# Attention and two expert layers on one core: two places for tokens that are transposed by DMA, some attention weights by DMA, and an order solved anew

## The chip, the cores and the metric

The kernel runs on one core of a Trainium2 chip. The metric is device time in microseconds from the start to the end of one execution. Runs of the kernel before took 1227.68 to 1228.92 us, with a median of 1227.95 us (3 runs).

## The reference, cut to what matters

```python
def _attn_ref(q, k, v):                    # (8, 8, 576, 64) each
    q_c, k_c, v_c = (x.reshape(8, 8, 9, 64, 64) for x in (q, k, v))     # chunks of 64 positions
    scores = 1.0 / np.sqrt(64) * np.matmul(q_c, k_c.transpose(0, 1, 2, 4, 3))
    attn = np.exp(scores - np.max(scores, axis=-1, keepdims=True))
    attn = attn / (np.sum(attn, axis=-1, keepdims=True) + 1e-09)
    return np.matmul(attn, v_c)            # reshaped to x, (4608, 512)

def _moe_ref(x, w_in, w_out, g_ln):        # w_in (512, 1024), w_out (1024, 512)
    h = x @ w_in
    e = np.exp(h - np.max(h, axis=-1, keepdims=True))
    solu = h * e / (np.sum(e, axis=-1, keepdims=True) + 1e-09)
    mu = np.mean(solu, axis=-1, keepdims=True)
    var = np.mean((solu - mu) ** 2, axis=-1, keepdims=True)
    return ((solu - mu) / np.sqrt(var + 1e-06) * g_ln) @ w_out

def _moe2_ref(x, w_in, w_out):             # w_in (512, 2048), w_out (2048, 512)
    h = x @ w_in
    return (h / (1.0 + np.exp(-h))) @ w_out
```

The three are applied one after the other. Inputs of the attention are 32-bit floats; the weights of the two layers arrive as 64-bit floats.

## The kernel before

**Two stages.** The first stage computes the attention and the first layer for 36 tiles of 128 rows, called tokens here and numbered from 0. The second stage computes the second layer by a scheme of seven products (`p1` to `p7`) instead of eight, for 6 groups of 768 rows: first its input product (336 `product` steps), then its output product (168 `out_product` steps). Every 32-bit operand is split into a high and a low part, and each product runs three passes (`PASSES`).

**One token in the first stage.** `attend(t)` (L556) multiplies token t's weights with its values and computes the scores of token t + 2; both go into the single `sx` tile in PSUM. ScalarE and VectorE split the attention result into `xs` (L607, L609). `weigh` (L582) turns scores into weights: maximum, difference, exponential, sum, a POOL multiplication (L596), then four TensorE transposes into `pp` (L600) and a copy to `pT` (L603). `moe_in` (L633) computes the 1024 columns of h in two halves of 12 matmuls; the PSUM tile `h` has one place. `hold` copies h to SBUF for the tokens that `HELD` marks (H), so that the place comes free. `norm` (L650) makes the normalised `u` in eight instructions, of which the last is L675.

**Turning a token.** The output product needs u transposed, as `lnT`, high and low. `turn_ln` (L677) does it with two groups of four TensorE transposes into `tp` (L683) and a split of each. `turn_x` (L688) does it for the 24 tokens that `XBAR` marks: a POOL copy takes the 16-bit halves of the words apart (L691), a transposing DMA follows (L694), a VectorE copy joins the halves (L697), and the split fills `lnT`. Each of its three buffers has one place, so tokens go through one behind the other. Four tokens make a block; `moe_out` (L704) computes the block's output in eight halves of 12 matmuls (`yp`), which are stored to DRAM as `y1d`.

**Weights.** `convert` (L486) turns 64-bit floats into 32-bit ones by integer operations: a scaling of the high word (on VectorE or ScalarE by `SCALE_ON`, L464, L466), a shift (L468) and two combinations (L470, L472). Pieces 0 to 7 are the first layer's weights, 8 to 23 the second layer's, which POOL mixes (L533) and SP stores. `LOW_ON` sets the engine of each low part; E is a subtraction by TensorE (L479, L480).

**What sets the order.** `stage_one` and `stage_two` describe every step with an engine, a length, needs, places and a due time. `Steps.solve` lists them by rank on each engine. The instructions are then issued in that order, and each engine, with SP for all DMAs, works through its queue in order. Tables of numbers at the end of the file (due times `FIRST`, `WAY_OUT`, `START`; engines) feed it.

```python
        pp = ps.tile([128, HP, 128], F32, tag="tr", name="pp", bufs=2)
        for hp in range(HP):
            nc.tensor.transpose(pp[:, hp, :], e[:, hp, :, :].rearrange("p h k -> p (h k)"), ident)
```

## Time and profile before

| | |
|---|---|
| median of 3 runs | 1227.95 us |
| the profiled execution | 1228.68 us |
| its span, first to last instruction | 1226.8 us |
| TensorE (PE) busy | 1187.6 us, 97% |
| VectorE (DVE) busy | 815.3 us, 66% |
| ScalarE (ACT) busy | 615.7 us, 50% |
| GpSimd (POOL) busy | 535.5 us, 44% |
| DMA | 257.31 MB, mean 210 GB/s |
| mean granted clock of TensorE | 0.992 |

Busy times are unions over an engine's instructions. The first product of the second stage starts at 504.72 us; from 527.6 us on TensorE runs second-stage products only.

### The profile page before, as it was taken

Reading aid. Unit: us, or ns where it says so; the run is one execution under the profiler, and the core shown is the slowest. Engines: PE = TensorE matmul, PEld = TensorE weight load, DVE = VectorE, ACT = ScalarE, POOL = GpSimd, SP = SyncE. Lnnn points to the kernel's source line nnn. Section 1 sums busy time; section 2 is a strip of 40 time slices with the busy share of each in tenths; the row PEclk is TensorE's granted clock in tenths of the full one; section 3 lists DMA queues with packets and bytes.
Section 4 is the critical chain, followed back from the end, with each engine's and each line's share of the span. In section 5 each row is a group of like instructions: output and inputs, shape, how many; then the busy total and the mean of one; then the engine's idle time right before and its main releaser. Section 6 shows DMA issues by size and latency. Waiting matters only on the chain.

```text
span 1226.8 us, 22015 instructions
## 1 busy us (share of the span) xinstructions
PE 1187.6 (97%) x8310; PEld 1093.5 (89%) x8310; DVE 815.3 (66%) x1119; ACT 615.7 (50%) x947; POOL 535.5 (44%) x510
## 2 busy tenths in 40 slices
PE   4999999898999999999999999999999999999998
PEld 2777778787888787899999999999999999999998
DVE  7987887887887865647565656566676555555553
ACT  4687545544555555654353435346655444444441
POOL 2344456455564642657667667578950000000000
PEclk9999999998999999999999999999999999999999
DMA  9444557758677653375757575659998777777772
GB/s 366 141 136 145 168 174 236 201 173 233 188 228 206 196 136 120 121 247 191 259 180 256 180 255 188 232 183 334 315 302 284 215 215 214 217 210 218 228 210 87
DMA packets 187177, 257.31 MB, mean 210 GB/s; under 512 B 64704, under 2 KB 142528, under 8 KB 187072
## 3 DMA queue, kind: packets, MB, share of 16 engines
q1 hardware_dynamic: 187072, 255.91, 67.0%
q8 instruction: 65, 1.06, 0.4%
q14 instruction: 40, 0.33, 0.1%
HBM read 143.66 MB, written 99.61 MB: 198 GB/s over the span
## 4 chain that ended last, share of the span: by engine, by line
PE 87%; DVE 6%; ACT 2%; DMA 2%; POOL 1%; issue 1%; SPq 0%; POOLq 0%; DVEq 0%
PE hyw L838 16%; PE hyw L926 16%; PE yp L710 13%; PE h L617 12%; PE h L838 12%; PE h L926 12%; PE sx L568 1%; DMA qk<-in_qk_dram 1%; PE sx L575 1%; DVE lnT L609 1%; DVE st L654 1%; PE tp L683 1%; DVE work L470 1%; PE pp L600 1%; DMA w2d<-work 1%
## 5 line engine op out<-in xcount | busy, mean ns | idle before, releaser
L912 DVE TENSOR_TENSOR gs<-gs 128x768 fp32r<-128x768 f32 x168 | 167.7, 1004 | 135.1 <-ACT gs L910 134.9
L910 ACT ACTIVATE gs<-gs 128x768 fp32r<-128x768 f32 x168 | 142.7, 849 | 176.5 <-PE hyw L926 82.5
L710 PE MATMUL yp<-lnT,wo 128*128 128x512 f32 x864 | 216.7, 400 | 3.8 <-DVE lnT L609 3.8
L617 PE MATMUL h<-wi,xs 128*128 128x512 f32 x864 | 216.8, 401 | 2.7 <-DVE u L660 1.7
L838 PE MATMUL hyw<-y1s,w2t 128*128 128x384 f32 x1152 | 214.6, 336 | 0.0
L926 PE MATMUL hyw<-gs,w2o 128*128 128x384 f32 x1152 | 211.5, 335 | 0.0
L838 PEld LDWEIGHTS hyw<-y1s,w2t 128*128 128x128 f32 x1152 | 202.0, 188 | 0.2
L926 PEld LDWEIGHTS hyw<-gs,w2o 128*128 128x128 f32 x1152 | 201.6, 188 | 0.0
L617 PEld LDWEIGHTS h<-wi,xs 128*128 128x128 f32 x864 | 162.3, 191 | 39.7 <-PE sx L575 1.7
L710 PEld LDWEIGHTS yp<-lnT,wo 128*128 128x128 f32 x864 | 162.4, 191 | 38.5 <-DVE lnT L609 4.5
L885 POOL TENSOR_TENSOR work<-work 128x384 f32<-128x384 f32 x144 | 161.1, 1139 | 76.2 <-ACT work L880 64.0
L838 PE MATMUL h<-y1s,w2t 128*128 128x384 f32 x864 | 164.5, 335 | 0.0
L926 PE MATMUL h<-gs,w2o 128*128 128x384 f32 x864 | 161.2, 336 | 0.0
L838 PEld LDWEIGHTS h<-y1s,w2t 128*128 128x128 f32 x864 | 151.7, 188 | 0.3
L926 PEld LDWEIGHTS h<-gs,w2o 128*128 128x128 f32 x864 | 151.1, 188 | 0.0
L596 POOL TENSOR_TENSOR e<-e,sm 128x512 f32<-128x512 f32 x36 | 51.2, 1423 | 59.9 <-DVE sm L594 53.8
L852 DVE TENSOR_TENSOR work<-hyw,work 128x384 f32<-128x384 f32 x48 | 26.7, 556 | 58.5 <-PE hyw L838 58.0
L533 POOL TENSOR_TENSOR work<-work 128x256 f32<-128x256 f32 x64 | 55.7, 888 | 20.0 <-DVE work L472 15.7
L864 ACT ACTIVATE work<-work 128x384 f32<-128x384 f32 x48 | 25.1, 524 | 77.8 <-DVE work L862 77.5
L672 POOL TENSOR_TENSOR st<-st,nhalf 128x1 f32<-128x1 f32 x36 | 33.0, 916 | 68.0 <-DVE st L670 67.6
L885 DVE TENSOR_TENSOR work<-work 128x384 f32<-128x384 f32 x48 | 49.3, 1034 | 14.9 <-POOL work L885 14.9
L675 ACT ACTIVATE u<-u,st 128x1024 f32<-128x1024 f32 x36 | 44.8, 1245 | 24.9 <-POOL st L673 24.9
(100 smaller groups left out, 1442.4 us busy)
## 6 DMA issues: line engine op xcount, KB each, us to landing
gd<-work SPq DMA_DIRECT2D x336, 192.0 KB, 2.3
gs<-gd SPq DMA_DIRECT2D x168, 384.0 KB, 3.8
qk<-in_qk_dram SPq DMA_DIRECT2D x36, 512.0 KB, 4.9
work<-in_w_out_dram SPq DMA_DIRECT2D x10, 1024.0 KB, 5.6
vt<-in_v_dram SPq DMA_DIRECT2D x36, 256.0 KB, 3.9
y1d<-work SPq DMA_DIRECT2D x36, 256.0 KB, 2.4
out_dram<-work SPq DMA_DIRECT2D x48, 192.0 KB, 4.1
work<-in_w_in_dram SPq DMA_DIRECT2D x8, 1024.0 KB, 5.1
```

The costliest lines, as they stand in the source:

```text
L533: nc.gpsimd.tensor_tensor(out=out_, in0=in0, in1=in1, op=op)
L596: nc.gpsimd.tensor_tensor(out=e, in0=e, in1=sm.to_broadcast([128, HP, 2, CH]), op=ALU.mult)
L617: nc.tensor.matmul(h, xs[:, a, kk // 2, 128 * (kk % 2):128 * (kk % 2) + 128], wi[b][kk // 2][:, kk % 2, n * 512:(n + 1) * 512], start=(kk ...
L672: nc.gpsimd.tensor_tensor(out=rs, in0=rs, in1=nhalf, op=ALU.pow)
L675: nc.scalar.activation(out=u, in_=u, func=AF.Identity, bias=off, scale=rs)
L710: nc.tensor.matmul(yp, wo[a][f // 4][:, f % 4, 128 * m:128 * (m + 1)], lnT[b][c][:, f, :], start=(f == 0 and i == 0), stop=(f == K1 - 1 an ...
L838: nc.tensor.matmul(acc, wt[j, o][:, a, kk, :], sy[o, c][:, kk, :], start=start and kk == 0 and n == 0, stop=kk == 1 and n == 2, skip_group ...
L852: nc.vector.tensor_tensor(out=take((u, "u3")), in0=bank[u, "y"], in1=c_t[u, "u2"], op=ALU.add)
L885: (nc.vector if T_ON[n] == "D" else nc.gpsimd).tensor_tensor(out=out, in0=in0, in1=in1, op=ALU.subtract)
L910: nc.scalar.activation(out=dst[:, 0], in_=src, func=AF.Copy)
L912: nc.vector.tensor_tensor(out=dst[:, 1], in0=src, in1=dst[:, 0].bitcast(F32), op=ALU.subtract)
L926: nc.tensor.matmul(acc, w[:, a, 128 * i:128 * i + 128], g[:, c, k, :], start=start and kp == 0 and k == 0 and n == 0, stop=kp == NF // 2 - ...
```

## The change

- **Tokens by DMA** (`turn_by_dma` for `turn_x`): the table `LN_BY` marks 26 tokens instead of 24. There are two places of 1024 words in `work`; a place takes the halves, the DMA writes the turned halves back over `u`, the join goes into the place again, and the place comes free after the split. The halves are taken apart on POOL for 21 tokens (P) and on ScalarE for 5 (A). `u` has four places instead of three.
- **Weights by DMA**: the table `P_BY` marks 9 tokens whose attention weights skip TensorE. The halves go to one of two places `ep` (POOL for 4, VectorE for 3, ScalarE for 2), a transposing DMA writes back over `e`, and ScalarE joins them into `pT`. `qk` has two places instead of three.
- **Conversion**: for 9 of 24 pieces `SCALE_ON` has L: ScalarE scales both words, and VectorE has two combinations left. Before there were 12 D and 12 A, now 8 D, 7 A and 9 L. The staging areas in `work` are moved. `LOW_ON` has three E instead of two.
- **Held tokens**: five of six are B, computed by `half_in` in two halves in the `y` banks, each copied to SBUF by itself.
- **The tables**: due times and engine choices are other numbers. In the second stage `T_ON` puts the last two of four differences (`g_sum`, L885) on VectorE, where the second one was alone before. `solve` keeps its ready steps in heaps; its rule of choice is the same.

```diff
-               ("PE", 0.45, dict(take=["tr"])), ("ACT", 0.59, dict(take=["pT"], free=["tr", "e"], give=[("p", n)])))
+               *([("PE", 0.45, dict(take=["tr"])), ("ACT", 0.59, dict(take=["pT"], free=["tr", "e"], give=[("p", n)]))] if P_BY[n] == "-" else
...
+                  ("ACT", 1.04, dict(take=["pT"], free=["e"], give=[("p", n)]))]))
...
-            st = work[:, 4096:6144].rearrange("p (k f) -> p k f", k=2)
+            st = work[:, 2048:4096].rearrange("p (k f) -> p k f", k=2)
...
+        if P_BY[t] != "-":
+            if "ep" not in early:
+                early["ep"] = sb.tile([128, 2, 512], F32, tag="ep", name="ep", bufs=1)
+            n = ep_free.pop(0)
+            x, e2 = early["ep"][:, n], e.rearrange("p a h k -> p (a h k)").bitcast(U16)
+            halves_apart(P_BY[t], x, e2)
+            yield
+            nc.sync.dma_start_transpose(out=e2.rearrange("p (m r) -> p m r", r=128), in_=x.bitcast(U16))
+            ep_free.append(n)
+            yield
+            p_t[t] = sb.tile([128, HP, 2, CH], F32, tag="pT", name="pT", bufs=2)
+            nc.scalar.activation(out=p_t[t].rearrange("p a c s -> p (a c s)").bitcast(U16).rearrange("p (n h) -> p n h", h=2),
+                                 in_=e2.rearrange("p (h n) -> p n h", h=2), func=AF.Copy)
+            return
...
-        u = sb.tile([128, 2, 512], F32, tag="u", name="u", bufs=3)
+        u = sb.tile([128, 2, 512], F32, tag="u", name="u", bufs=4)
...
-    def turn_x(t):
+    def turn_by_dma(t):
         b, tt = divmod(t, BT)
...
+        n = x_free.pop(0)
+        x = work[:, n:n + 1024]
+        u = ln.pop(t).rearrange("p a f -> p (a f)").bitcast(U16)
+        halves_apart("PA"[LN_BY[t] in "AJ"], x, u)
+        yield
+        nc.sync.dma_start_transpose(out=u.rearrange("p (m r) -> p m r", r=128), in_=x.bitcast(U16))
+        yield
+        halves, joined = u.rearrange("p (h n) -> p n h", h=2), x.bitcast(U16).rearrange("p (n h) -> p n h", h=2)
...
+            nc.vector.tensor_copy(out=joined, in_=halves)
         yield
...
+        yield from split(hi, lo, x.rearrange("p (m r) -> p m r", r=128))
+        x_free.append(n)
+
+    x_free = [4096, 5120]
...
-T_ON = 'PDPP'
+T_ON = 'PPDD'
...
-HELD = '-HHHHHH-----------------------------'
-LOW_ON = 'PEEDDDDPPPPDPDDD'
-SCALE_ON = 'DAAAADDDAADDAADDDDADADAA'
-XBAR = '--------XXXXXXXXXXXXXXXXXXXXXXXX----'
+HELD = 'HB-BBB-B----------------------------'
+LOW_ON = 'EEEPDDDPPDPDPDPP'
+SCALE_ON = 'DAALLALDDDLDALLADALLDADL'
+LN_BY = '------AAPA-PPPPPPAPPPPPPPPPP-PPP-PA-'
+P_BY = '------------D---D---------PPP--AAP-D'
```

**The order, first place: the start.** SP's queue from its first load on, before:

```order
L431 DMA st_e<-in_w_in_dram 128x2x1024 x2
L550 DMA qk<-in_qk_dram 128x1024
L431 DMA st_e<-in_w_in_dram 128x2x1024
L550 DMA qk<-in_qk_dram 128x1024
L431 DMA st_e<-in_w_in_dram 128x2x1024
L550 DMA qk<-in_qk_dram 128x1024
L554 DMA vt<-in_v_dram 128x512 x2
L431 DMA work<-in_w_out_dram 128x2x1024
L431 DMA st_e<-in_w_out_dram 128x2x1024 x2
L544 DMA gsb<-in_g_ln_dram 128x8x1
L550 DMA qk<-in_qk_dram 128x1024 x2
```

and now:

```order
L439 DMA st_e<-in_w_in_dram 128x2x1024 x2
L559 DMA qk<-in_qk_dram 128x1024 x2
L439 DMA st_e<-in_w_in_dram 128x2x1024 x2
L563 DMA vt<-in_v_dram 128x512 x2
L439 DMA work<-in_w_out_dram 128x2x1024
L439 DMA st_e<-in_w_out_dram 128x2x1024 x2
L553 DMA gsb<-in_g_ln_dram 128x8x1
L559 DMA qk<-in_qk_dram 128x1024 x3
```

Seven loads of weights (`st_e`, `work`) and two of values stand ahead of the third `qk` load, which stood ahead of the values before. On TensorE, from the scores of token 2 on, before (`sx<-qk` are scores, `sx<-pT,vt` the attention result, `pp` transposed weights, `h` the first layer's product):

```order
L575 MATMUL sx<-qk 64x64 x16
L600 MATMUL pp<-ident,e 128x128 x4
L617 MATMUL h<-wi,xs 128x512 x12
L568 MATMUL sx<-pT,vt 64x64 x16
L575 MATMUL sx<-qk 64x64 x16
L617 MATMUL h<-wi,xs 128x512 x12
L600 MATMUL pp<-ident,e 128x128 x4
L568 MATMUL sx<-pT,vt 64x64 x16
L575 MATMUL sx<-qk 64x64 x16
L600 MATMUL pp<-ident,e 128x128 x4
L617 MATMUL h<-wi,xs 128x512 x12
L568 MATMUL sx<-pT,vt 64x64 x16
```

and now (`hp` is a half of h in a `y` bank):

```order
L584 MATMUL sx<-qk 64x64 x16
L642 MATMUL h<-wi,xs 128x512 x12
L577 MATMUL sx<-pT,vt 64x64 x16
L584 MATMUL sx<-qk 64x64 x16
L642 MATMUL h<-wi,xs 128x512 x12
L642 MATMUL hp<-wi,xs 128x512 x12
L625 MATMUL pp<-ident,e 128x128 x4
L642 MATMUL hp<-wi,xs 128x512 x12
L625 MATMUL pp<-ident,e 128x128 x4
L577 MATMUL sx<-pT,vt 64x64 x16
L584 MATMUL sx<-qk 64x64 x16
L577 MATMUL sx<-pT,vt 64x64 x16
```

The two `pp` groups have moved ahead of the first attention result, and two attention steps now stand directly behind each other: the scores of one, then the attention result of the next.

**Second place: around tokens 22 and 23.** TensorE before, ending with the attention result of token 23 (`yp` is the first layer's output product):

```order
L617 MATMUL h<-wi,xs 128x512 x12
L600 MATMUL pp<-ident,e 128x128 x4
L710 MATMUL yp<-lnT,wo 128x512 x12
L568 MATMUL sx<-pT,vt 64x64 x16
L575 MATMUL sx<-qk 64x64 x16
L710 MATMUL yp<-lnT,wo 128x512 x12
L617 MATMUL h<-wi,xs 128x512 x12
L600 MATMUL pp<-ident,e 128x128 x4
L617 MATMUL h<-wi,xs 128x512 x12
L600 MATMUL pp<-ident,e 128x128 x4
L568 MATMUL sx<-pT,vt 64x64 x16
L575 MATMUL sx<-qk 64x64 x16
```

and now, from the attention result of token 22 to that of token 23:

```order
L577 MATMUL sx<-pT,vt 64x64 x16
L584 MATMUL sx<-qk 64x64 x16
L642 MATMUL h<-wi,xs 128x512 x12
L749 MATMUL yp<-lnT,wo 128x512 x12
L625 MATMUL pp<-ident,e 128x128 x4
L749 MATMUL yp<-lnT,wo 128x512 x12
L642 MATMUL h<-wi,xs 128x512 x12
L577 MATMUL sx<-pT,vt 64x64 x16
L584 MATMUL sx<-qk 64x64 x16
L642 MATMUL h<-wi,xs 128x512 x12
L749 MATMUL yp<-lnT,wo 128x512 x24
```

A `pp` group stood right ahead of the attention result and two stood close together; now two products stand between a group and the next attention result, and an h product and two output products lie between two h tiles.

**Third place: the end of the first stage.** TensorE before, from the last token's first half of h up to the output products that start the last block:

```order
L617 MATMUL h<-wi,xs 128x512 x12
L683 MATMUL tp<-ident,u 128x128 x4
L617 MATMUL h<-wi,xs 128x512 x12
L710 MATMUL yp<-lnT,wo 128x512 x12
L683 MATMUL tp<-ident,u 128x128 x4
L710 MATMUL yp<-lnT,wo 128x512 x12
L683 MATMUL tp<-ident,u 128x128 x4
L710 MATMUL yp<-lnT,wo 128x512 x12
L683 MATMUL tp<-ident,u 128x128 x4
L710 MATMUL yp<-lnT,wo 128x512 x12
L683 MATMUL tp<-ident,u 128x128 x4
L710 MATMUL yp<-lnT,wo 128x512 x24
```

and now, to the first products of the second stage (L877):

```order
L749 MATMUL yp<-lnT,wo 128x512 x24
L642 MATMUL h<-wi,xs 128x512 x12
L749 MATMUL yp<-lnT,wo 128x512 x12
L642 MATMUL h<-wi,xs 128x512 x12
L749 MATMUL yp<-lnT,wo 128x512 x36
L708 MATMUL tp<-ident,u 128x128 x8
L749 MATMUL yp<-lnT,wo 128x512 x12
L877 MATMUL h_5046<-y1s,w2t 128x384 x6
L749 MATMUL yp<-lnT,wo 128x512 x12
L877 MATMUL h_5082<-y1s,w2t 128x384 x6
```

The last token's transposes (`tp`) stood apart, one group between two output products; now both groups stand together, three output products behind the last h product and directly ahead of the last block's first one.

## Rows read from the trace of the kernel before

**Rows 1.** Stretches: us, busy time by engine, clock, DMA share, GB/s

```profile
9.69:22.27 12.58, 7.75 (x143) 4.71 (x143) 12.34 (x19) 7.61 (x10) 4.70 (x3) 1.00 1.03 408
22.27:60.35 38.08, 32.90 (x383) 25.85 (x381) 35.50 (x59) 24.51 (x37) 14.40 (x17) 0.96 0.56 196
60.35:138.49 78.14, 75.21 (x837) 61.17 (x835) 64.79 (x106) 56.88 (x89) 34.67 (x47) 1.00 0.45 143
138.49:504.72 366.23, 353.16 (x2855) 286.62 (x2849) 279.44 (x389) 198.21 (x290) 189.60 (x214) 0.98 0.67 190
...
527.62:1226.80 699.18, 695.64 (x3997) 695.32 (x3995) 407.45 (x538) 317.75 (x505) 279.49 (x216) 1.00 0.72 228
...
527.00:870.00 343.00, 343.00 (x1971) 342.88 (x1970) 210.96 (x308) 161.47 (x302) 244.81 (x192) 1.00 0.69 232
```

**Rows 2.** Timeline of TensorE: start, length, instructions, [wait ahead, releaser]

```profile
243.96 4.34 PE L710 MATMUL yp<-lnT,wo 128*128 128x512 f32 x11 [1.90 <-DVE lnT L609]
...
292.75 1.14 PE L568 MATMUL sx<-pT,vt 64*64 64x64 f32 x32 [3.57 <-DVE xs L609]
...
295.12 7.75 PE L617 MATMUL h<-wi,xs 128*128 128x512 f32 x24 [0.37 <-DVE u L660]
...
407.82 0.69 PE L568 MATMUL sx<-pT,vt 64*64 64x64 f32 x32 [2.55 <-issue]
...
409.07 4.41 PE L710 MATMUL yp<-lnT,wo 128*128 128x512 f32 x12
...
462.05 4.03 PE L710 MATMUL yp<-lnT,wo 128*128 128x512 f32 x11 [1.94 <-DVE lnT L609]
```

**Rows 3.** Timeline of TensorE, one transposing group among products

```profile
330.43 2.90 PE L710 MATMUL yp<-lnT,wo 128*128 128x512 f32 x12
333.17 0.60 PE L600 MATMUL pp<-ident,e 128*128 128x128 f32 x4
333.52 3.01 PE L710 MATMUL yp<-lnT,wo 128*128 128x512 f32 x12
336.37 2.91 PE L617 MATMUL h<-wi,xs 128*128 128x512 f32 x12
```

**Rows 4.** Timeline of TensorE, first h product and fourth scores

```profile
22.27 0.70 PE L617 MATMUL h<-wi,xs 128*128 128x512 f32 x2
...
29.72 0.69 PE L575 MATMUL sx<-qk 64*64 64x64 f32 x32 [0.61 <-DMA qk<-in_qk_dram]
```

**Rows 5.** Timeline of SP, issue of two query-key loads

```profile
16.12 8.47 SPq L550 DMA_DIRECT2D qk<-in_qk_dram  x2
```

**Rows 6.** Timeline of TensorE, last h product and last transposes

```profile
483.56 3.02 PE L617 MATMUL h<-wi,xs 128*128 128x512 f32 x12
...
495.59 0.60 PE L683 MATMUL tp<-ident,u 128*128 128x128 f32 x4
```

**Rows 7.** Timeline of ScalarE, u of the last token

```profile
493.50 1.24 ACT L675 ACTIVATE u<-u,st 128x1024 f32<-128x1024 f32 x1
```

**Rows 8.** Groups by line: turning a token by DMA; busy, mean ns

```profile
L691 POOL COPY work<-u 128x2048 uint16<-128x2048 uint16 x24 | 51.7, 2156 | 11.3 <-ACT u L675 11.3
...
L609 DVE TENSOR_TENSOR lnT<-xb,lnT 128x1024 fp32r<-128x1024 f32 x24 | 39.7, 1653 | 12.6 <-ACT lnT L607 12.5
...
L697 DVE COPY xb<-work 128x2048 uint16<-128x2048 uint16 x24 | 34.5, 1438 | 0.6 <-DMA work<-work 0.6
...
L607 ACT ACTIVATE lnT<-xb 128x1024 fp32r<-128x1024 f32 x24 | 25.4, 1056 | 18.0 <-DVE xb L697 17.9
```

**Rows 9.** DMA issues: count, median us to landing

```profile
work<-work SPq DMA_TRANSPOSE x24, 4.4
```

**Rows 10.** Timeline of VectorE, split behind those transposes

```profile
496.86 0.69 DVE L609 TENSOR_TENSOR lnT<-tp,lnT 128x512 fp32r<-128x512 f32 x1 [0.87 <-ACT lnT L607]
```

**Rows 11.** Groups by line: differences on VectorE in the second stage

```profile
L885 DVE TENSOR_TENSOR work<-work 128x384 f32<-128x384 f32 x48 | 49.3, 1034 | 14.9 <-POOL work L885 14.9
```

**Rows 12.** Waits of SP: us in total, times, longest

```profile
SPq L554 <- PE sx L568: 86.8, 22, 11.0
```

More of the change, by code (lines that the diff above doesn't have):

```diff
@@ L86, in solve, with is_ready @@
         engines = sorted({st["engine"] for st in self.steps})
-        ready, free_at, places = {e: [] for e in engines}, {e: 0.0 for e in engines}, self.places
+        ready, free_at, places, count = {e: {} for e in engines}, {e: 0.0 for e in engines}, self.places, 0
+        def is_ready(st):
+            nonlocal count
+            count += 1
+            key = () if st["engine"] == "DMA" else tuple(sorted(st["take"]))
+            heapq.heappush(ready[st["engine"]].setdefault(key, []), (0.0 if st["engine"] == "DMA" else st["rank"], count, st))
         for st in self.steps:
             if not st["left"]:
-                ready[st["engine"]].append(st)
+                is_ready(st)
         loaded = {place for st in self.steps if st["engine"] == "SP" for place in st["take"]}
-        events, count, mode, port = [(0.0, 0, None, 0)], 0, 0, {"DVE": 0.0, "POOL": 0.0}
+        events, mode, port = [(0.0, 0, None, 0)], 0, {"DVE": 0.0, "POOL": 0.0}
         while events:
@@ L108, in solve @@
                     continue
-                if e == "DMA":
-                    st = ready[e][0] if ready[e] else None
-                else:
-                    st = min((st for st in ready[e] if all(places[p] >= st["take"].count(p) for p in st["take"])), key=lambda st: st["rank"], default=None)
-                if st is None:
+                kind = min((take for take, heap in ready[e].items() if heap and all(places[p] >= take.count(p) for p in take)),
+                           key=lambda take: ready[e][take][0][:2], default=None)
+                if kind is None:
                     continue
-                ready[e].remove(st)
+                st = heapq.heappop(ready[e][kind])[2]
                 for place in st["take"]:
@@ L434, in conv_load @@
         if q < 8:
-            cv = work[:, 1024 * (q % 4):1024 * (q % 4) + 1024].rearrange("p (k f) -> p k f", k=2)
+            n = (0, 1024, 4096, 5120)[q % 4]
+            cv = work[:, n:n + 1024].rearrange("p (k f) -> p k f", k=2)
         else:
@@ L701, in turn_x, with halves_apart @@
         hi, lo = (y[:, :, 128 * tt:128 * (tt + 1)] for y in lnT[b])
-        yield from split(hi, lo, x)
+        yield from split(hi, lo, x.rearrange("p (m r) -> p m r", r=128))
+        x_free.append(n)
+    x_free = [4096, 5120]
+    def halves_apart(on, out, src):
+        out, src = out.bitcast(U16).rearrange("p (h f) -> p h f", h=2), src.rearrange("p (f h) -> p h f", h=2)
+        if on == "A":
+            nc.scalar.activation(out=out, in_=src, func=AF.Copy)
+        else:
+            (nc.vector if on == "D" else nc.gpsimd).tensor_copy(out=out, in_=src)
     def moe_out(b, m):
```

63 lines of the change are left out of this document (31 added, 32 removed).

## The prediction

> **What bounds the kernel now.** I read the stretches of TensorE first, then its timeline, then what the waits end on. TensorE is busy nearly throughout [rows 1]: from 527.6 us to the end it loses 699.2 - 695.6 = 3.5 us, from 504.7 to 527.6 nothing, so the second stage is TensorE's own work and only less work there would shorten it. Before that it is idle 5.2 us from 22.3 to 60.4, 2.9 us up to 138.5 and 13.1 us up to 504.7. A wait costs more than itself: the granted clock of the last of these stretches is 0.98 of 2.4 GHz, so part of it ran at 1.2 GHz, and the timeline shows where [rows 2]. After 1.9 us of idling eleven matmuls of an output product take 4.34 us, where twelve take 2.90 [rows 3]: 1.7 us lost. The same comparison gives 0.45 + 1.95 us (an attention step 1.14 where as many matmuls take 0.69 [rows 4], 24 matmuls 7.75 where two products take 5.8) after the 3.57 us wait, 1.5 after 2.55, 1.4 after 1.94: 7.0 us in all. Two percent of 366 us is 7.3, so both readings agree. What can be won ahead of 504.7 us is thus TensorE work, plus 13.1 + 7.0 = 20.1 us of waits after 138.5 us, plus 8.1 us before.
>
> **TensorE work removed.** Nine groups of four transposes of weights (36 to 27) and four groups for tokens (12 tokens by two to 10 by two) leave TensorE. One group costs the difference of two steps [rows 3]: an output product to its successor is 2.74 us, the transposes and the product behind them 3.20, so 0.46 us. 13 x 0.46 = **-6.0 us**, on the path because TensorE ends last. The extra fp32 subtraction (three instead of two "cl" pairs) lies in the wait for loads at the start, so zero; without that cover it costs less than a product step of 2.74 us, which is twelve matmuls of its width.
>
> **The start.** SP now sends the third query-key load behind seven weight loads, the fourth one already had that place. In this trace TensorE gets the fourth at 29.72 us [rows 4], although SP issued the pair from 16.1 us on [rows 5]: the transfers move 408 GB/s at a DMA share of 1.03 [rows 1], so it stands in a full queue. With one 0.5 MB load less ahead, the third now lands 0.52/0.408 = 1.3 us earlier than the fourth did, at 28.4 us. TensorE's order has its scores ahead of the first h product, so that product starts at 28.4 + 0.7 = 29.1 us instead of 22.3: +6.8 us (bounds: nothing, if the load overtakes; +8.1 if it lands where the fourth did). The Trainium skill, page "DMA: Bandwidth & Descriptors", section "Where 436 GB/s comes from", holds that an HBM load is bound at about 358 GB/s per core; by that the load would land some 3 us later and the sum be 3 us worse. No trace of this case bears that out: 408 GB/s stands in the row.
> Against this stand the 8.1 us that TensorE waited between 22.3 and 138.5 us, mostly for data that VectorE prepares. VectorE starts on its conversions as early as before and so is 6.8 us further along when products begin. I take 2 us of them to remain (bounds 0 and 8.1). New is an attention step that stands directly behind another one (end of the first place in the order): both use the single sx tile, and ScalarE and VectorE must read it in between. Its wait lies between nothing and the 3.6 us of the longest such wait [rows 2]; I take 2.5, the shorter row, with 1.5 us of low clock behind it. Sum of the start: 6.8 - 8.1 + 2 + 4 = **+4.7 us**.
>
> **The steady part, 138 to 505 us.** Each long wait ends on VectorE: the xs split (3.57 us, and behind "issue" 2.55 us) or the lnT split (1.9 and 1.94) [rows 2]. The new order leaves more room at both places. Between a block's last h product and the block's first output product stood six or seven products; now there are nine each time, so 2 x 2.74 = 5.5 us more less one or two transposing groups. What must fit is one DMA-turned token: 8.2 us from h to u (product ends at 483.56 + 3.02, u at 493.50 + 1.24 [rows 6, 7]), POOL copy 2.16, DMA 4.4, join 1.44, ScalarE 1.06, split 1.65 [rows 8, 9]: 18.9 us, with nine products alone 24.7. Weights transposed two at a time right ahead of an attention step are gone as well; each now has two products behind it. VectorE itself is relieved little: nine conversions put word scaling on ScalarE and drop their shift, four of them a scaling too, but two more tokens need join and split (2 x 3.1 us) in place of four short splits, and three weight copies come on. So hiccups stay possible. I keep 6.0 us: one wait with its low clock (1.9 + 1.7), 1.2 for small ones, and 1.2 at the end (next). Before 20.1, now 6.0: **-14.1 us** (bounds -20.1 + 1.2 and 0).
>
> **The end of the first stage.** Token 35's two transposing groups now stand three products (8.2 us) behind its last h product, which is just when u is ready. Straight behind them comes the last block's first output product, which needs the split of the first half. In this trace that took from 495.59 to 496.86 + 0.69 = 497.55 us, 1.96 us [rows 6, 10]; the second group covers 0.8, so 1.2 us wait (already counted; up to 1.9 + 1.4 if it goes as at 462 us [rows 2]).
>
> **The second stage.** Two of four differences move from POOL to VectorE: 48 more of 1.03 us [rows 11], 50 us on top of the 211 us that VectorE is busy in 527 to 870 us [rows 1]: 261 of 343 us, 76%. About eight products stand between a bank's last product and its next use, so the cost is **0**; without that cover the 50 us would be an upper bound. POOL loses the same 48.
>
> **Sum.** -6.0 + 4.7 - 14.1 = -15.4 us. The profiled execution took 1228.7 us (span 1226.8), so 1213.3; the median of the runs is 0.7 below it, so **1212.6 us**. A measurement of this kernel can tell about 0.2%, 2.5 us, from no change.
>
> **Rivals.**
> VectorE keeps its hiccups. Its joins average 1.44 us and its splits 1.65 [rows 8], and it has 279 us of work in the 366 us [rows 1]. If waits after 138.5 us are as long as before, the steady term is 0: 1228.7 - 6.0 + 4.7 - 0.7 = **1226.7 us**. For it: VectorE's load per token hardly falls while TensorE's period does. Against it: the order gives each of the four kinds of wait more slack. Chance 0.20. The Trainium skill, page "SBUF — State Buffer", section "Who interferes with whom", says that of a two-port VectorE copy and a POOL instruction the first holds the shared port for its whole length; by that a join can lose a whole POOL copy. Means above the shortest instructions agree with it, and the rival stands without it.
> SP holds transposes back, and it gets slower. SP works in order. A load of values or of queries and keys waits for TensorE to free its place, and SP spent 86.8 us that way, up to 11.0 at once [rows 12]; query-key places fall from three to two, and transposes of weights join the queue. The point that decides: a block's last transpose must lose more than 24.7 - 18.9 = 5.8 us in queues (somewhat more with the attention steps between). Then seven blocks (2 to 8) start late by a wait like that at 243.96 us, 1.9 + 1.7 us each [rows 2]: +25.2, or **1237.8 us**. Against it: only two waits of this kind exist now, with less room. Chance 0.15.
> No new wait at all: the two attention steps pass freely, early waits vanish, nothing but the 1.2 us at the end remains: 1213.3 - 4 - 2 - 4.8 - 0.7 = **1201.8 us**. Chance 0.10.
> That the change doesn't do what it says is excluded for TensorE by its order: the groups are gone there.
>
> **How the numbers follow.** The forecast has 0.55. Its own bounds are some 1205 (early waits gone, one hiccup fewer) and 1224 (early waits as before, two more hiccups). The range 1204 to 1230 takes in the forecast and the VectorE rival, and leaves out the slow one and most of the best. Faster by over 0.2%: 0.55, 0.10 and a quarter of the VectorE case, 0.70. Within 0.2%: most of that case, 0.12. Slower: 0.15 and the tails, 0.18.
>
> **What would show it.** The first h product at about 29 us behind a wait for qk; a wait of some 2.5 us between the third and fourth attention steps; 108 "pp" and 80 "tp" matmuls; between 138 us and the first L877 product some 5 us of waits instead of 13; L877 and out products without waits. A first h product at 22 us, waits on lnT at most block starts, or any wait above 2 us in the second stage would make it wrong.

## The result, and the profile after

The changed kernel takes 1214.09 us, median of 4 runs (1211.97 to 1216.71), beside 1228.43 us for the kernel before on the same chip. The ratio is 0.9881, with a 95% interval of 0.9858 to 0.9905: faster by 1.2%. A second set of runs, beside the experiments, gave 1214.37 us and 0.9885 (0.9867 to 0.9903). The profiled execution has a span of 1212.2 us, 14.6 less than before. In the code after, the h product is L642 (before L617), the output product L749 (L710), an attention step L577 and L584 (L568 and L575), the split L634 (L609), u L685 (L660).

The stretches of the changed kernel, as in [rows 1]: length, busy time and count of each engine, mean granted clock, DMA share, GB/s.

```profile
core 0: us, PE busy (x) PEld busy (x) DVE busy (x) ACT busy (x) POOL busy (x), PEclk, DMA share, GB/s
9.57:28.31 18.74, 9.56 (x114) 5.54 (x114) 17.39 (x21) 12.79 (x16) 6.63 (x4) 0.85 0.99 376
28.31:143.11 114.80, 110.11 (x1173) 89.97 (x1173) 99.09 (x161) 86.52 (x133) 49.95 (x65) 0.94 0.51 149
143.11:486.06 342.95, 338.68 (x2862) 273.81 (x2861) 255.35 (x371) 213.24 (x297) 174.71 (x218) 1.00 0.75 210
515.86:1212.20 696.34, 692.24 (x3973) 690.90 (x3971) 425.34 (x584) 314.81 (x503) 224.74 (x166) 1.00 0.72 228
```

From the first output product of block 1 (143.11 us) to the first L877 product (486.06) TensorE loses 342.95 - 338.68 = 4.3 us, and the clock column reads 1.00; before it lost 13.1 us in the matching stretch, at 0.98 [rows 1]. VectorE is busy 255 of 343 us there, 74%, where it was 279 of 366, 76%.

The timeline of TensorE at the start, and of SP's queue:

```profile
21.89 0.69 PE L577 MATMUL sx<-pT,vt 64*64 64x64 f32 x32
28.31 1.13 PE L584 MATMUL sx<-qk 64*64 64x64 f32 x32 [5.72 <-DMA qk<-in_qk_dram]
30.16 5.49 PE L642 MATMUL h<-wi,xs 128*128 128x512 f32 x12 [0.72 <-ACT xs L632]
...
51.18 1.14 PE L577 MATMUL sx<-pT,vt 64*64 64x64 f32 x32 [3.72 <-ACT e L600]
52.05 1.11 PE L584 MATMUL sx<-qk 64*64 64x64 f32 x32
53.10 4.69 PE L642 MATMUL h<-wi,xs 128*128 128x512 f32 x12
```

```profile
13.43 16.40 SPq L559 DMA_DIRECT2D qk<-in_qk_dram  x3
```

The third query-key load lands at 28.3 us and TensorE waits 5.7 us for it. The first h product starts at 30.16 where it stood at 22.27 [rows 4]. The fourth attention step, directly behind the third, waits 3.72 us. The h products behind these waits take 5.49 and 4.69 us for twelve matmuls, where 2.9 is usual.

The end of the first stage answers to [rows 6]: three short waits, 1.5 us in all.

```profile
481.09 1.09 PE L708 MATMUL tp<-ident,u 128*128 128x128 f32 x8 [0.72 <-ACT u L700]
482.44 0.49 PE L749 MATMUL yp<-lnT,wo 128*128 128x512 f32 x1 [0.25 <-ACT lnT L632]
483.42 2.79 PE L749 MATMUL yp<-lnT,wo 128*128 128x512 f32 x11 [0.49 <-DVE lnT L634]
```

The groups of transposes that are left on TensorE (busy us, mean ns, idle time before them):

```profile
L625 PE MATMUL pp<-ident,e 128*128 128x128 f32 x108 | 16.3, 273 | 3.5 <-POOL e L607 3.5
L708 PE MATMUL tp<-ident,u 128*128 128x128 f32 x80 | 12.1, 275 | 1.0 <-ACT u L700 0.7 <-ACT pT L628 0.2
```

And what TensorE waited for in the second stage, where it waited for nothing before (us in total, times, longest):

```profile
PE hyw L965 <- DVE work L990: 0.6, 1, 0.6
PE h L965 <- DVE gs L951: 0.2, 1, 0.2
```

In the steady part the order now repeats one cadence. This is TensorE's timeline there:

```profile
285.74 2.91 PE L642 MATMUL h<-wi,xs 128*128 128x512 f32 x12
288.58 0.69 PE L577 MATMUL sx<-pT,vt 64*64 64x64 f32 x32
289.10 0.65 PE L584 MATMUL sx<-qk 64*64 64x64 f32 x32
289.67 3.04 PE L642 MATMUL h<-wi,xs 128*128 128x512 f32 x12
292.55 5.61 PE L749 MATMUL yp<-lnT,wo 128*128 128x512 f32 x24
298.00 2.91 PE L642 MATMUL h<-wi,xs 128*128 128x512 f32 x12
```

One half of a token's h product, the next attention step, the other half, two output products, then the next token's h. For every token from 13 to 35 exactly two output products stand between the last h product of the token before and its own first one. In the kernel before it is two for 16 of these tokens, one for six (13, 17, 25, 29, 30, 34) and none for token 21; there stands the longest wait of the steady part, at 292.75 us [rows 2]. The forecast had not counted this; the experiments led to it.

### The profile page after: what moved, and what is told of

It reads as the page before. It is cut to its first block, busy times and chain, and to the rows that moved or that the text cites. A ratio compares the mean times of both kernels' runs of the same rounds, so it can differ in the third digit from the quotient of the medians.

```text
span 1212.2 us, 21948 instructions
## 1 busy us (share of the span) xinstructions
PE 1180.4 (97%) x8261; PEld 1086.5 (90%) x8261; DVE 817.5 (67%) x1151; ACT 642.4 (53%) x972; POOL 472.5 (39%) x468
## 4 chain that ended last, share of the span: by engine, by line
PE 88%; DMA 4%; DVE 4%; ACT 2%; issue 1%; POOL 1%; SPq 0%; DVEq 0%; ACTq 0%; POOLq 0%
PE hyw L877 16%; PE hyw L965 15%; PE yp L749 14%; PE h L642 13%; PE h L877 12%; PE h L965 11%; PE hp L642 2%; DMA gs<-gd 2%; PE sx L577 2%; PE sx L584 1%; DVE gs L951 1%; PE pp L625 1%; PE tp L708 1%; DMA qk<-in_qk_dram 1%; DMA u<-work 1%
## 5 line engine op out<-in xcount | busy, mean ns | idle before, releaser
L877 PE MATMUL hyw<-y1s,w2t 128*128 128x384 f32 x1152 | 215.4, 336 | 0.0
L749 PE MATMUL yp<-lnT,wo 128*128 128x512 f32 x864 | 209.8, 394 | 0.7 <-DVE lnT L634 0.5
L877 PEld LDWEIGHTS hyw<-y1s,w2t 128*128 128x128 f32 x1152 | 201.9, 188 | 0.7 <-DVE work L891 0.3
L749 PEld LDWEIGHTS yp<-lnT,wo 128*128 128x128 f32 x864 | 159.9, 188 | 34.5 <-DVE lnT L634 0.8
L642 PE MATMUL h<-wi,xs 128*128 128x512 f32 x744 | 188.2, 403 | 2.6 <-DVE u L685 1.8
L642 PEld LDWEIGHTS h<-wi,xs 128*128 128x128 f32 x744 | 140.0, 192 | 35.0 <-issue 3.5
L877 PE MATMUL h<-y1s,w2t 128*128 128x384 f32 x864 | 164.8, 335 | 0.0
L924 POOL TENSOR_TENSOR work<-work 128x384 f32<-128x384 f32 x96 | 108.6, 1147 | 115.0 <-ACT work L919 114.2
L877 PEld LDWEIGHTS h<-y1s,w2t 128*128 128x128 f32 x864 | 151.7, 188 | 0.3
L924 DVE TENSOR_TENSOR work<-work 128x384 f32<-128x384 f32 x96 | 75.0, 803 | 0.0
L607 POOL TENSOR_TENSOR e<-e,sm 128x512 f32<-128x512 f32 x36 | 41.8, 1162 | 74.6 <-DVE sm L605 56.5
L679 DVE TENSOR_REDUCE st<-h 128x1 f32<-128x1024 f32 x30 | 36.3, 1212 | 31.4 <-PE h L642 31.4
```

Of the source, the lines that this page charges most:

```text
L607: nc.gpsimd.tensor_tensor(out=e, in0=e, in1=sm.to_broadcast([128, HP, 2, CH]), op=ALU.mult)
L642: nc.tensor.matmul(h, xs[:, a, kk // 2, 128 * (kk % 2):128 * (kk % 2) + 128], wi[b][kk // 2][:, kk % 2, n * 512:(n + 1) * 512], start=(kk ...
L679: nc.vector.tensor_reduce(out=mx, in_=h, axis=AX.XY, op=ALU.max, negate=True)
L749: nc.tensor.matmul(yp, wo[a][f // 4][:, f % 4, 128 * m:128 * (m + 1)], lnT[b][c][:, f, :], start=(f == 0 and i == 0), stop=(f == K1 - 1 an ...
L877: nc.tensor.matmul(acc, wt[j, o][:, a, kk, :], sy[o, c][:, kk, :], start=start and kk == 0 and n == 0, stop=kk == 1 and n == 2, skip_group ...
L924: (nc.vector if T_ON[n] == "D" else nc.gpsimd).tensor_tensor(out=out, in0=in0, in1=in1, op=ALU.subtract)
```

## The experiments

Theory at the outset: an edit is worth the TensorE time that it removes, the start loses to the late load, and the steady part gains because the order leaves room, not because VectorE has less to do. The rivals are those of the prediction. Medians below stand each beside runs of the kernel before on the same chip, 1228.8 to 1229.7 us. "Wait" below is what TensorE was not busy from 143.11 to 470 us, taken from the windows of each trace.

**The changed kernel again**, as the measure for the set.

> The changed kernel once more, so that the other kernels of this set have it beside them on the same chip. Its four runs lay between 1212.0 and 1216.7 us, 0.9881 of the kernel before. Theory and rivals alike: a median of 1214 us (1212 to 1216.5), a ratio between 0.986 and 0.9905.

Measured: 1214.37 us, ratio 0.9885 (0.9867 to 0.9903), span 1212.4, wait 2.8 us as in the first trace.

**Weights back on TensorE, nothing else moved.**

```diff
+    for t in range(36):
+        if P_BY[t] != "-":
+            when = times["weigh", t]
+            times["weigh", t] = when[:4] + [when[6] - 0.6, when[6]]
...
-        if P_BY[t] != "-":
+        if False:
```

> The nine groups of transposes of weights go back from DMA to TensorE; each stands about where ScalarE joined the halves, and the place of every other instruction in every engine's order stays. Theory (TensorE ends last everywhere, an edit is worth the TensorE time that it removes): 9 x 0.46 = 4.1 us more, 1218.2 us beside 1214.1. First rival (the transposing DMAs for weights cost more on SP and its queue than they save): 0 to 2 us more, or less time than the changed kernel. Second rival (they also gave the vector engines the room that removed the waits after 138 us): waits of 2 to 4 us come back in that stretch and it takes 8 us more or worse, 1222 us.

Measured: 1219.70 us, ratio 0.9938 (0.9918 to 0.9959); the spans of the two profiled executions differ by 1217.0 - 1212.4 = 4.6 us, the medians by 5.3. The wait from 143 to 470 us is 1.7 us, less than in the changed kernel. So the nine groups cost 0.5 to 0.6 us each and no wait came back: the theory's 4.1 us is right in kind and a little short.

**The nine shifts back on VectorE, in two ways.** In the first the order of every engine is kept, in the second the planner is told and solves it anew.

```diff
-        if SCALE_ON[q] == "L":
+        if False:
...
-SCALE_ON = 'DAALLALDDDLDALLADALLDADL'
+SCALE_ON = 'DAAAAAADDDADAAAADAAADADA'
```

> The nine conversions with word scaling on ScalarE get their shift on VectorE back; every order stays otherwise. That is 9 x 0.82 = 7.4 us more on VectorE, three of them (2.5 us) before 60 us, and 9 x 1.15 = 10 us less on ScalarE. Theory (the waits after 138 us went because the order has nine products where six or seven stood, not because VectorE has less to do): at most the 2.5 us at the start, so 1214 to 1216.6 us, and the wait total from the first output product of block 1 to the last h product stays below 6 us (4.3 in the changed kernel). Rival (VectorE's load sets the waits): the waits on lnT or xs come back, at least four of 1.9 us with 1.7 us of low clock each, 14 us, 1228 us.

> The same nine shifts on VectorE as in shift_dve, but told to the planner, which then solves the whole order anew: the same work on every engine, another order. Between a block's last h product and its first output product stand 10, 11, 10, 8, 8, 6, 7, 6, 2 products (blocks 0 to 8) where the changed kernel has 10, 13, 9, 9, 9, 9, 9, 9, 3. Theory (the order's slack at the block starts removed the waits): waits on lnT or on a split come back at some of the blocks with 6 to 8, 1.9 us with 1.7 us of low clock each; two to five of them, so 1221 to 1232 us. Rival (the slack there isn't what decides, since shift_dve has the same work and took no longer): 1212 to 1216.5 us.

Measured: 1214.40 us with the order kept (0.9884, 0.9866 to 0.9902; wait 3.7 us), 1229.80 us with the order solved anew (1.0012, 1.0000 to 1.0025; wait 10.9 us). Both have the same instructions on every engine, nine shifts more on VectorE than the changed kernel (VectorE is busy 823.8 us in place of 817.5 with the order kept). All 15.4 us between the two are the order. Waits came back, but not at the block starts, where the theory had them. In the solved-anew kernel TensorE stands at attention steps:

```profile
344.60 1.13 PE L577 MATMUL sx<-pT,vt 64*64 64x64 f32 x32 [3.39 <-issue]
...
451.13 0.69 PE L577 MATMUL sx<-pT,vt 64*64 64x64 f32 x32 [1.96 <-issue]
453.46 4.58 PE L642 MATMUL h<-wi,xs 128*128 128x512 f32 x12 [1.64 <-DVE u L685]
```

These are the steps of tokens 27 and 35. Its order has no output product between the h products of tokens 24 and 25, and none between those of 32 and 33: exactly where these two steps stand.

**One place for transposing DMAs; and the old choice of tokens and weights**, both solved anew.

```diff
-    step = Steps(dict(S=1, X=1, tr=2, y=2, h=1, u=4, xs=2, e=2, pT=2, qk=2, v=2, ln=2, ys=2, hs=4, x=2, ep=2))
+    step = Steps(dict(S=1, X=1, tr=2, y=2, h=1, u=4, xs=2, e=2, pT=2, qk=2, v=2, ln=2, ys=2, hs=4, x=1, ep=2))
-    x_free = [4096, 5120]
+    x_free = [4096]
```

> One place for transposing DMAs of tokens in place of two, order solved anew; the work of every engine is that of the changed kernel. The products between a block's last h product and its first output product become 10, 14, 9, 8, 7, 6, 7, 6, 2. Theory (the second place is what lets the planner leave nine products): waits on lnT at two to five block starts, 1.9 + 1.7 us each: 1221 to 1232 us. Rival (one place is busy some 11 us of a token's 11.6 and suffices): 1212 to 1216.5 us.

```diff
-LN_BY = '------AAPA-PPPPPPAPPPPPPPPPP-PPP-PA-'
-P_BY = '------------D---D---------PPP--AAP-D'
+LN_BY = '--------PPPPPPPPPPPPPPPPPPPPPPPP----'
+P_BY = '------------------------------------'
```

> The tokens and weights that the kernel before gave to DMA (24 tokens, no weights), with two places, four u buffers, the halves of h and the tables of the change; order solved anew: 10, 14, 10, 9, 7, 7, 7, 6, 4 products at the block starts. Theory: the thirteen transposing groups come back, 13 x 0.46 = 6.0 us, and waits at two to four of the block starts with 6 or 7, 3.6 us each: 1227 to 1234 us, about the kernel before. Rival (all of the steady part's gain came from the two places and the tables and none from these choices): 1220 us.

Measured: one place 1233.15 us (1.0041, 1.0027 to 1.0055), wait 16.6 us, above both ranges, and none of its waits between 143 and 470 us is on lnT, where the theory had them; the old choice 1224.42 us (0.9968, 0.9957 to 0.9980), wait 7.6 us, between theory and rival. Here too the waits stand where the cadence breaks. With one place there are four such tokens, 21, 25, 29 and 33, and the steps of tokens 23, 27, 31 and 35 waited 2.24, 1.96, 4.85 and 1.96 us, with up to 3.32 us more for the h place behind them:

```profile
400.13 1.13 PE L577 MATMUL sx<-pT,vt 64*64 64x64 f32 x32 [4.85 <-issue]
...
454.17 0.69 PE L577 MATMUL sx<-pT,vt 64*64 64x64 f32 x32 [1.96 <-issue]
458.19 4.88 PE L642 MATMUL h<-wi,xs 128*128 128x512 f32 x12 [3.32 <-DVE u L685]
```

| kernel | tokens 13 to 35 with no output product ahead of their h | with one | wait 143 to 470 us | median us |
|---|---|---|---|---|
| changed | none | none | 2.8 | 1214.1 |
| shift_dve | none | none | 3.7 | 1214.4 |
| old_parts | 29, 33 | 21, 25 | 7.6 | 1224.4 |
| shift_new | 25, 33 | 29 | 10.9 | 1229.8 |
| before | 21 | six | 13.1 | 1228.4 |
| one_place | 21, 25, 29, 33 | none | 16.6 | 1233.2 |

At all nine tokens of the second column the attention step there waited, 1.8 to 4.9 us; no attention step of the changed kernel in this stretch waited over 0.9 us. Why such a place waits can be read from what the instructions need: the end of an h product gives up an xs place and fills the one h place. Only then can the copy and split of the next xs run, on which the attention step waits, and the maximum, the exponential and u, on which the next h product waits. With two output products between, TensorE has 5.5 us of other work for them.

Counted by that need, the six orders agree more sharply than by the cadence. With two xs places, an attention step needs the end of the h product of the token three before it. Ten steps stand with no product behind that end: the nine of the table and token 32's in the kernel before (2.55 us [rows 2]). All ten waited, 1.8 to 4.9 us. The other 133 steps of the six kernels in this stretch have at least one product there, and none of them waited over 0.94 us. The changed order has no step of the first kind. This is how order and waits go together; the next kernels ask whether such a place alone makes the wait.

**Is a product more at that place enough?** Two kernels move only output products on TensorE.

```diff
+    for b, m, k, t in (3, 3, 1, 23),:          # before_swap
+    for b, m, k, t in (3, 3, 1, 23), (4, 3, 1, 27), (5, 3, 1, 31), (6, 3, 0, 35):   # one_place_swap
+        y, shift = times["moe_out", b, m], times["attend", t][0] - 0.5 - times["moe_out", b, m][k]
+        times["moe_out", b, m] = y[:k] + [when + shift for when in y[k:]]
```

> The kernel before, with one output product moved three places down: the second half of block 3's last one, from ahead of the first h product of token 20 to behind the second, where the attention step of token 23 stood right behind that h product (one transposing group between). No other instruction changes its place, no work changes. Theory (what cost time in the kernel before was the order of TensorE: an attention step with no product between it and the h product that gives up its xs place must wait for copy, split and step): the wait of 3.57 us there, the 0.4 us behind it and the 2 us of low clock go, up to 1 us comes for the h product of token 20, which now stands closer to the one before it: 5 to 6 us less, 1222 to 1224 us, beside 1228.4 to 1228.9. Rival (VectorE is late at that point whatever the order, or the wait comes back at the next attention step): 1227 to 1230 us.

> The kernel with one place for transposing DMAs (1233.2 us), with one output half-product each moved a place or two down so that it stands between an h product and the attention step behind it at tokens 23, 27, 31 and 35: those are the four steps with no product there, and the four that waited (2.24, 1.96, 4.85 and 1.96 us, 11 us in all, with 4 to 6.5 us of low clock behind them). Theory (the order decides, the second place only as far as it changes the order): 10 to 16 us less, 1217 to 1223 us. Rival (the second place is worth its 18.7 us in itself, one place being too few for transposing DMAs): the waits move to lnT or to the next step, 1229 to 1234 us.

Measured: before_swap 1227.36 us (0.9983, 0.9972 to 0.9994), 2.3 us less by the medians and 4.0 by the spans of the profiled executions, under the 5 to 6 expected and inside the rival's range; its wait is 12.9 us, where the kernel before had 13.1. one_place_swap 1231.70 us, 1.5 less by the medians and 3.7 by the ratios to the kernel before, where 10 to 16 were expected: a miss, and again inside the rival's range. In the first the attention step no longer waits, but the transposes ahead of it do:

```profile
287.50 1.11 PE L600 MATMUL pp<-ident,e 128*128 128x128 f32 x4 [2.48 <-POOL e L596]
```

In the second the steps of tokens 27 and 35 pass, but the h product behind the latter waits 3.57 us, and the steps of 23 and 31 still wait 2.70 and 4.18. Their splits come late because VectorE and ScalarE, each in its own order, stand for a transfer (VectorE and ScalarE rows of the timeline, with what they waited for):

```profile
285.55 0.69 DVE L473 TENSOR_SCALAR work<-work 128x1024 f32<-128x1024 f32 x1 [5.35 <-DMA w2d<-work]
...
393.17 1.17 ACT L620 ACTIVATE pT<-e 128x1024 uint16<-128x1024 uint16 x1 [1.80 <-DMA e<-ep]
```

A conversion that waits until the stores of an earlier one's weights (w2d) have left its area, and a join of weights whose transposing DMA is late, hold the split behind them. The second already stands in one_place, ahead of its longest wait, the 4.85 us: ScalarE stood 2.02 us for the same kind of DMA there, with the copy of xs next in its order. One product shifted repairs neither. So no product at that place goes with a wait each time, and a product at that place doesn't by itself remove it.

**Or is it VectorE's order alone?** The last kernel moves five of its instructions in the kernel before.

```diff
+    times["convert", 16][1:4] = [286.5, 286.6, 286.7]
+    times["attend", 22][2] = 286.3
```

> The kernel before, with five instructions of VectorE in another order: at token 22 the split that the attention step of token 23 waits for, and the maximum behind it, stand ahead of three steps of a w2 conversion (3.5 us in that trace) instead of behind them. TensorE's order and all work stay. Theory (the waits of the kernel before sit where VectorE, in its own order, is busy with conversions while the split behind them is due; the change removed them by another order of that engine as much as of TensorE): the wait of 3.57 us falls below 1.5, the 2 us of low clock behind it go, a little comes back later: 3 to 5 us less in the profile, 1224 to 1226 us beside 1228.9 to 1229.7. Rival (only room on TensorE helps, since ScalarE's copy ahead of the split and the weights from POOL come late too, as the 2.5 us wait for POOL in before_swap says): the wait stays above 2 us, no more than 1 us less.

Measured: 1230.07 us, ratio 1.0005 (0.9995 to 1.0015): no gain, as the rival had it. The split came early and the wait fell from 3.57 to 0.98 us, as the theory had it, but the next wait took its place:

```profile
289.87 0.69 PE L568 MATMUL sx<-pT,vt 64*64 64x64 f32 x32 [0.98 <-DVE xs L609]
290.38 0.65 PE L575 MATMUL sx<-qk 64*64 64x64 f32 x32
296.07 7.53 PE L617 MATMUL h<-wi,xs 128*128 128x512 f32 x24 [5.05 <-DVE u L660]
```

With no output product between two tokens' h, the second waits until u has been computed out of the one h place. That chain (maximum, exponential, u) and the conversions that now stand inside it fill the time. Neither of these moves on one engine helped by itself.

**The third query-key load early.** SP issues it ahead of three loads of w_out, and the steps that use it move up in the orders of the other engines.

```diff
+    times["load_qk", 2] = [10.2]
+    for q, when in (6, 10.5), (4, 10.9), (5, 11.3):
+        times["convert", q][0] = when
+    times["attend", 0] = [21.2, 23.3, 24.0]
+    times["moe_in", 0][0] = 24.05
+    times["weigh", 2][:4] = [24.5, 26.0, 29.75, 31.0]
+    times["attend", 1] = [28.0, 30.0, 31.0]
+    times["weigh", 3][:4] = [31.75, 33.0, 33.8, 34.9]
```

> The third query-key load is issued ahead of three loads of w_out, and the first two attention steps with tokens, the first h product and the third and fourth softmax stand some 6 us earlier in the orders; nothing else moves. Theory (the start lost its time to that load): the wait of 5.7 us for qk before the first h product goes, that product starts at 23 to 25 us instead of 30.2, and 2 to 4 us of the 5.8 that the start lost come back: 1210 to 1212 us. What holds it from more is that VectorE's conversions set when the second h product can start. Rival (VectorE's conversions set the start anyhow, and the wait for the load only hid that): the first h product starts early, the same time is waited behind it, and the run takes 1213 to 1216 us.

Measured: 1210.63 us (0.9857, 0.9835 to 0.9879), 3.7 us less, as expected. The first h product starts at 24.44 us; part of the gain is given back at the fourth attention step, whose wait grows from 3.7 to 5.0 us:

```profile
24.44 3.31 PE L642 MATMUL h<-wi,xs 128*128 128x512 f32 x12 [0.71 <-ACT xs L632]
...
29.52 0.69 PE L584 MATMUL sx<-qk 64*64 64x64 f32 x32 [1.15 <-DMA qk<-in_qk_dram]
...
47.08 1.13 PE L577 MATMUL sx<-pT,vt 64*64 64x64 f32 x32 [5.01 <-ACT e L600]
```

**One difference of the second stage back on POOL.**

```diff
-T_ON = 'PPDD'
+T_ON = 'PDPP'
```

> One of the two differences of the second stage that went to VectorE goes back to POOL (PDPP for PPDD, as in the kernel before); the first stage's order stays. Theory (the second stage lost 1.3 us because VectorE is nearer to its limit there): waits on VectorE's work and gs after 515 us, 0.8 us in the changed kernel, go, and 1 to 1.3 us come back: 1213 us, within the uncertainty of 2 us, so the profile's waits and the length from the last output product on decide. Rival (the second stage lost nothing to VectorE): the same waits, or longer ones on POOL, and 1214 to 1216 us.

Measured: 1211.58 us (0.9863, 0.9845 to 0.9881). TensorE has no wait for VectorE's work or gs left after 515 us. From the last output product of the first stage to the end it takes 695.3 us, where the five traces with PPDD and the same first stage have 696.2 to 696.9: 0.9 to 1.6 us. The next kernel, with the same edit, has 695.8. The rest of the 2.8 us between the medians lies in the first stage, where nothing was changed; executions of the changed kernel lie 4.7 us apart, so it is not put down to the edit.

**The gains joined**, with a third edit at the fourth attention step.

```diff
+    times["weigh", 2][4:] = [38.5, 38.58]
+    times["attend", 2][1:] = [44.5, 45.25]
+    times["moe_in", 2] = [47.4, 51.3]
```

> The changed kernel with the two edits that gained (the third query-key load early, one difference of the second stage back on POOL) and a third: at the third attention step with a token, ScalarE's copy and VectorE's split stand ahead of a conversion and of the next softmax, the first h product of token 2 stands ahead of the fourth attention step instead of behind it, and the weights' copy for token 2 ahead of a conversion. Theory (two edits 3.7 and 1.2 to 2.8 us less; the third removes the wait of 5.0 us between those steps, of 1.1 us ahead of them and 1 us of low clock, and leaves 1 to 2 us for the split behind the fourth step, so 4 to 6 less): 1202 to 1206 us. Rival (VectorE's conversions bound the start, and the wait only moves behind the fourth step): 1207 to 1210 us.

Measured: 1207.41 us, 5 runs (1206.34 to 1209.24), ratio 0.9819 (0.9803 to 0.9834): the fastest of the study, 7 us less than the changed kernel and 1.8% less than the kernel before. It is 1.4 us above what was expected, and inside the rival's 1207 to 1210, which is not excluded. The wait of 5.0 us is gone; 1.45 and 0.37 us came ahead of token 2's h product and 1.3 us before token 4's, and the first h product ran slow:

```profile
24.17 5.49 PE L642 MATMUL h<-wi,xs 128*128 128x512 f32 x12 [0.72 <-ACT xs L632]
...
42.77 0.74 PE L642 MATMUL h<-wi,xs 128*128 128x512 f32 x2 [1.45 <-ACT xs L632]
43.88 2.56 PE L642 MATMUL h<-wi,xs 128*128 128x512 f32 x10 [0.37 <-DVE xs L634]
...
61.16 2.57 PE L642 MATMUL hp<-wi,xs 128*128 128x512 f32 x10 [1.31 <-DVE xs L634]
```

## Why the prediction was right

The forecast was 1212.6 us and the median is 1214.1. Its terms, against the two profiled executions:

| term | forecast | measured |
|---|---|---|
| TensorE work removed | -6.0 | -6.0 by count; the nine groups of weights alone 4.6 to 5.3 where 4.1 was said |
| the start | +4.7 | +5.7 |
| the steady part and its end | -14.1 | -15.8 |
| the second stage | 0 | +0.9 to +1.6 |
| sum | -15.4 | -14.6 in the span |

The total is nearer than its terms: the start and the second stage came out dearer by 1.0 and by 0.9 to 1.6 us, the steady part 1.7 us better, and these nearly cancel. That much of the agreement is luck.

**The groups** were right: 108 and 80 transposes are left, and weights_pe prices a group at 0.5 to 0.6 us, where 0.46 was read from the steps.

**The start** came as described, and somewhat dearer. The first output product of block 1 starts at 143.11 us, 4.6 later than before, with 1.1 us less work ahead of it on TensorE (six transposing groups of 0.46 and one attention step of 1.1 less, one product of 2.74 more), so 5.7 us are lost. The load landed at 28.3 us, 28.4 was forecast; the product behind it started at 30.16, not 29.1, because ScalarE's copy of xs stood behind conversions in its order (0.72 us) and the scores ran 1.13 us. The wait between the third and fourth attention steps was 3.72 us; the forecast took the shorter of two rows, and the longest of them, 3.57, was the right one. Of the 2 us of other early waits that the forecast kept, 1.0 stayed (0.72 and 0.25). The low clock was mis-sized: behind the two long waits it cost 5.49 - 2.9 and 4.69 - 2.9, 4.4 us in the h products alone, where 1.5 were counted. What it cost the kernel before in this stretch was not counted either: ten matmuls took 3.87 us there from 23.54 us on, some 1.4 too long. The terms then still add up to about 1 us more than the 5.7 that were lost, and what makes up the rest is open. The stretch from 9.57 to 28.31 us moved 376 GB/s at a DMA share of 0.99. The Trainium skill, page "DMA: Bandwidth & Descriptors", section "Where 436 GB/s comes from", has about 358 GB/s for a core as the bound; the trace lies above it, and by that figure the same bytes would have taken an estimated 0.9 us longer (18.74 x 376 / 358 = 19.7), not the 3 us that the prediction reckoned from 408 GB/s. qk_early shows that load and the orders behind it together cost 3.7 us; which of them held the first product longer was not tried apart.

**The steady part** was right in size and only half right in its reason. The forecast put the gain in the room that the order leaves, and against the rival that VectorE's load sets the waits; shift_dve gives VectorE nine shifts back, 6.3 us of busy time, without any effect, and shift_new, with the same work in another order, takes 15.4 us longer. That is shown. But the room was looked for above all in the nine products at a block's start. shift_new has six to eight there in blocks 3 to 7, as the kernel before, and no wait on lnT. And in the kernel before the room did not tell which block waits: its two waits on lnT stand at blocks with seven and eight products (the prediction read six or seven everywhere), while four others with six or seven waited nothing. What held those two splits is in the rows of VectorE, ScalarE and POOL before:

```profile
240.93 1.89 POOL L691 COPY work<-u 128x2048 uint16<-128x2048 uint16 x1
241.21 2.69 DVE L609 TENSOR_TENSOR lnT<-xb,lnT 128x1024 fp32r<-128x1024 f32 x1 [1.13 <-ACT lnT L607]
...
455.25 1.04 ACT L607 ACTIVATE lnT<-xb 128x1024 fp32r<-128x1024 f32 x1
459.04 1.23 DVE L654 TENSOR_REDUCE st<-h 128x1 f32<-128x1024 f32 x1 [5.03 <-PE h L617]
460.18 0.68 DVE L609 TENSOR_TENSOR xs<-sx,xs 128x512 fp32r<-128x512 f32 x1
460.78 1.22 DVE L609 TENSOR_TENSOR lnT<-xb,lnT 128x1024 fp32r<-128x1024 f32 x1
```

At 462 us the token was ready to be split from 456.3 us on; VectorE stood 5.03 us for an h product, because its order has that product's maximum and the xs split ahead. At 244 us the split itself ran 2.69 us, where the median is 1.24, beside a POOL copy. The first is order again, not room.

The step that failed is thus "what must fit is one DMA-turned token" as the reason for the waits. What the runs show in its place is that the order decides, and that the waits of the table stand where an attention step has no product between it and the h product that it needs: ten of ten such steps in four orders waited, and none of the 133 others over 0.94 us. That this trait alone makes the waits is not shown: moving one product or five VectorE instructions won 0 to 2.3 us (3.7 by the ratios in one_place_swap), two steps with a product moved in still waited 2.70 and 4.18 us, and a kernel with the changed one's order and a single broken cadence wasn't tried. Whether the second place is worth anything except through the order that it allows stays open too.

**The second stage** lost about 1 us where nothing was expected. The cover that was named, eight products between a bank's uses, was not the one that ended: TensorE waited 0.6 us for VectorE's work on an output and 0.2 us for gs, and diff_pool takes both away; joined, with the same edit, has one wait of 0.23 us left.

**The rivals.** VectorE keeps its hiccups (1226.7 us): refuted by the 4.3 us of waits that are left, and for this order by shift_dve too. SP holds transposes back (1237.8): the transposing DMAs of tokens land 4.8 us after their issue, where 4.4 stood in [rows 9], and VectorE's join waits for them 7.8 us in all, but TensorE never waited for a block's last one. The same mechanism does show on ScalarE and VectorE in one_place_swap, where a late transfer holds the split behind it; so it was the right thing to fear, in other orders than this one. No new wait at all (1201.8): the start rules it out, and joined, without two of those waits, is still 5.6 us above it.

## What to carry to other kernels

Where every engine works through its own order, count on the bottleneck engine how much work stands between the two uses of each single place (here one h place and two xs places) and leave no place with none: the ten such steps here waited 1.8 to 4.9 us each. That is a sign of a bad order and not a handle to mend it with: moving one product, or one engine's instructions, brought out the next wait behind it, because every engine has an order of its own. Before an edit in such a kernel is judged, run it once with the order held fixed: here the same edit cost 0 us with the order kept and 15.4 us with the order solved anew. And look at which load stands ahead of which in the first queue: one 0.5 MB load moved ahead of three others, with the steps that use it, gave 3.7 us.

## What the runs showed of the hardware

The same wait does not always bring the same clock. In qk_early the first h product starts after an idle stretch of 3.18 us and 0.71 us and takes 3.31 us; in joined TensorE idles 3.16 and 0.72 us at the same places and the same twelve matmuls take 5.49 us. From 24 to 30 us the granted clock is at its upper level, 2.4 GHz (1.00), in the first and at its lower one, 1.2 GHz (0.50), in the second:

```profile
24.00:30.00 6.00, 4.41 (x76) 3.13 (x76) 5.48 (x7) 4.91 (x6) 1.07 (x1) 1.00 0.93 365
24.00:30.00 6.00, 5.83 (x28) 4.17 (x32) 5.75 (x7) 4.94 (x6) 0.79 (x1) 0.50 0.92 361
```

Nothing in TensorE's two timelines ahead of it differs by more than 0.3 us, so what decides there is not seen in these rows. That is 2.2 us between two executions at a place where the two kernels don't differ.

In the kernel before a split on VectorE with both inputs in SBUF (L609, lnT from xb) took 1.24 us in the median of 24 and up to 2.91; the one of 2.69 us at 241.21 us had a POOL copy beside it. The 36 splits of xs, which read sx in PSUM, all took 0.67 to 0.69 us. No run here isolates the two causes, the place of the input and the POOL copy.
